# A hand-ordered attention and MLP block: another order for key sums, loads, scalings and weighings

## The chip, the cores and the metric

The kernel runs on one core of one Trainium2 chip. The metric is the time of one execution on the device in microseconds (us), the median of several runs. The core has five engines that run side by side, each working through its own instructions in order: TensorE (PE in the profile; its weight loads are PEld), VectorE (DVE), ScalarE (ACT), GpSimd (POOL) and SyncE (SP), which here only issues DMA transfers. They meet by semaphores.

## The reference

One token block of S = 2048 tokens and D = 576 features: a linear attention with 32 heads of 18 features, then an MLP with 4608 hidden features. All inputs are bf16.

```
x1 = layernorm(x)
q, k, v = heads(x1 @ wqkv)                       # 32 heads of 18
phi(t) = [softmax(t @ w_phi), softmax(-t @ w_phi)]     # 36 features a head
kv = sum over tokens of phi(k)^T v;   z = sum over tokens of phi(k)
o  = phi(q) kv / (phi(q) . z + 1e-6)
h  = x + o @ wo
y  = layernorm(layernorm(h))
out = h + gelu(y @ w1 + b1) @ w2 + b2
```

## The kernel before

**Tiles.** The 2048 tokens are 16 tiles of 128; two tiles make a pair p = 0 to 7, and the second index of most steps, i or a, picks a half of the heads or a tile of the pair. w_phi is folded into the key weights (wkp) and the query weights (wqp) on the chip, so that one product gives the logits.

**Order.** The scheduler is off: the body of the kernel is one long list of calls, and every engine runs its part of the list in the order in which it stands. So the list is at once the queue of each engine and of SP's DMA ring; an instruction that waits holds up all that stand behind it on its engine. TensorE's results go through a PSUM pool named `two` with three buffers in turn, so that a product can start only when the result three places back has been read.

**The steps that the change moves**, for a pair p:

- `load_x(t0, t1)`: SP loads tokens of x. `stats(p, i)`: VectorE's mean and variance. `power(p)`: GpSimd's 1/sqrt. `centre(p, i)`: GpSimd's shift, needed only where ACT scales. `scale(p, i, act or vec)`: the normalised tile, written by ACT (line 266) or VectorE (line 308). `turn_dma(p)`: SP transposes it by DMA (line 315) into lnT.
- `turn_wq(c)`: SP transposes chunk c of the query weights by DMA (line 368). `fold_mm("q", c)`, `fold_ev`: TensorE folds w_phi into it (line 393), ACT writes it to wqp (line 404). `swap_q(0 to 2)`: SP copies halves of wqp to the other 64 partitions (lines 408 to 412).
- `value_mm`, `key_mm`, `query_mm`: 18 matmuls each on 64 rows (line 423). `value_ev`: ACT's copy to vals (line 433). `key_exp`, `query_exp`: two exponentials each on ACT (line 445).
- `key_sum(p, i)`: VectorE's softmax denominators, a reduce and a reciprocal (lines 474, 476). `key_weigh(p, i, a, engine)`: phi(k) times the reciprocal (line 480), on GpSimd before. `query_sum`, `query_weigh`: the same for queries, into `padded` (lines 500 to 519). `turn_q(p)`: two DMA transposes of `padded` (line 545).
- `sums(p, a)`: eleven matmuls on 128 rows that add a tile's kv and z into `acc_kv` (line 559). All sixteen must be done ahead of `table`; `combine_mm` (line 644) then multiplies turned queries with the table, `divide` (lines 657, 658) divides.
- `load_wo(half)`: SP loads 64 partitions of wo (line 604), first used by `residual_mm` (line 693). `load_w1`, `load_w2`: the MLP's weights (lines 586, 592). The first quarter of w1 lies where the raw query and key weights lay.

SP's queue of before around the change is: `turn_dma(3)`, five `turn_wq`, `turn_dma(4)`, `load_x(12, 16)`, `turn_dma(5)`, `load_wo(0)`, three `swap_q`, two quarters' parts of w1, `turn_dma(6)`, `turn_dma(7)`, two parts of w1, `load_wo(1)`, `turn_q(0)`, and then w1 and w2 to the end.

After the attention of the first pair the MLP begins: `up` (line 1140, gelu in line 1162) and `down` (line 1184), with the later pairs' attention put between; the change leaves all that as it is.

Of the kernel before, what the change touches and what calls it, by code (L numbers as in the profile page):

```python
# [43 lines left out]
def kernel(  # L44
# [236 lines left out]
    def stats(p, i):  # L281
        if i == 0:
            moments[p] = [small.tile([P, 2, 2], FP32, name="mv", tag="mv")]
        mv = moments[p][0]
        st = small.tile([P, 2, nc.vector.BN_STATS_DIM], FP32, name="st", tag="st")
        for h in range(2):
            nc.vector.bn_stats(st[:, h, :], xh[:, 2 * p + i, h * HALF : (h + 1) * HALF])  # L287
        nc.vector.bn_aggr(mv[:, i, :], st[:, :, :])  # L288
        if i:
            moments[p] = [mv, None, None, None]  # L290

    def power(p):
        va = small.tile([P, 2], FP32, name="va", tag="va")
        nc.gpsimd.tensor_scalar(va[:, :], moments[p][0][:, :, 1], 1.0, EPS, ALU.mult, ALU.add)
        rs = small.tile([P, 2], FP32, name="rs", tag="rs")
        nc.gpsimd.tensor_tensor(rs[:, :], va[:, :], mhalf[:, 0:2], ALU.pow)
        moments[p][1] = rs
# [69 lines left out]
    def turn_wq(c):  # L367
        nc.sync.dma_start_transpose(wT[:, :, c * P : (c + 1) * P], wq[:, c, :])
# [119 lines left out]
    def key_sum(p, i):  # L488
        total("k", phik[p], p, i)

    def key_weigh(p, i, a, eng):
        weigh("k", phik[p], p, i, a, eng)
# [58 lines left out]
    def sums(p, a):  # L551
        t = 2 * p + a
        left.remove(t)
        for w in range(KW):
            n = COUNT[w]
            f0 = min(w * STEP, PW - P)
            b = w // 6
            at = (w - BANKS[b][0]) * WV
            nc.tensor.matmul(  # L559
                acc_kv[:, b, at : at + n * VW],  # L560
                phik[p][:, a, f0 : f0 + P],
                vals[:, t, FIRST[w] : FIRST[w] + n, :].rearrange("p h v -> p (h v)"),
                start=False, stop=not left, skip_group_check=True,
            )
# [285 lines left out]
    key_exp(1, 0)  # L850
    scale(3, 0, act)
    turn_dma(3)
    turn_wq(4)
    key_sum(0, 1)
    value_mm(0, 1)
    value_ev(0, 1, act)
    key_weigh(0, 0, 1, pool)
    key_weigh(0, 0, 0, pool)
    stats(4, 0)
    stats(4, 1)  # L860
    value_mm(1, 1)
# [2 lines left out]
    key_mm(2, 1)  # L864
    key_weigh(0, 1, 0, pool)
    key_weigh(0, 1, 1, pool)
    power(4)
    value_mm(1, 0)
    sums(0, 0)
    key_exp(2, 0)  # L870
    key_exp(2, 1)
    value_ev(1, 0, act)
    key_sum(2, 0)
    key_weigh(2, 0, 1, pool)
    stats(5, 0)
    stats(5, 1)
    power(5)
    scale(4, 1, vec)
    value_mm(2, 0)
    value_ev(2, 0, act)  # L880
    key_mm(1, 1)
    key_exp(1, 1)
    turn_wq(1)
    key_sum(2, 1)
    turn_wq(2)
    scale(4, 0, vec)
    centre(5, 1)
    scale(5, 1, act)
    value_mm(2, 1)
    value_ev(2, 1, act)  # L890
    key_mm(3, 0)
    key_exp(3, 0)
    value_mm(3, 0)
    key_weigh(2, 0, 0, pool)
    value_ev(3, 0, act)
    turn_wq(3)
    turn_wq(0)
    key_mm(3, 1)
    key_exp(3, 1)
    key_sum(1, 0)  # L900
    key_weigh(2, 1, 1, pool)
    sums(0, 1)
    value_mm(3, 1)
    turn_dma(4)
    value_ev(3, 1, act)
    fold_mm("q", 0)
    key_weigh(2, 1, 0, pool)
    key_weigh(1, 0, 1, pool)
    key_sum(1, 1)
    fold_ev("q", 0, act)  # L910
    sums(2, 0)
    key_weigh(1, 0, 0, pool)
    sums(2, 1)
    scale(5, 0, vec)
    key_weigh(1, 1, 1, pool)
    key_weigh(1, 1, 0, pool)
    key_sum(3, 1)
    fold_mm("q", 3)
    fold_ev("q", 3, act)
    load_x(12, 16)  # L920
    key_weigh(3, 1, 1, pool)
    fold_mm("q", 2)
    fold_ev("q", 2, act)
    stats(6, 0)
    key_sum(3, 0)
    key_weigh(3, 1, 0, pool)
    turn_dma(5)
    load_wo(0)
    value_mm(4, 1)
    value_ev(4, 1, act)  # L930
    fold_mm("q", 1)
    fold_ev("q", 1, act)
    key_weigh(3, 0, 1, pool)
    key_weigh(3, 0, 0, pool)
# [3 lines left out]
    key_exp(4, 0)  # L938
    key_sum(4, 0)
    power(6)  # L940
    fold_mm("q", 4)
    swap_q(2)
    fold_ev("q", 4, act)
    swap_q(0)
    key_mm(4, 1)
    sums(1, 0)
    key_exp(4, 1)
    key_sum(4, 1)
# [3 lines left out]
    key_mm(5, 1)  # L952
    key_exp(5, 0)
    key_exp(5, 1)
    key_sum(5, 1)
    load_w1(0, 4, syn)
    sums(3, 1)
    centre(6, 1)
    value_mm(4, 0)
    value_ev(4, 0, act)  # L960
    query_mm(0, 0)
    scale(6, 1, act)
    value_mm(5, 0)
    centre(6, 0)
    scale(6, 0, act)
    key_weigh(4, 0, 0, pool)
    key_weigh(4, 1, 1, pool)
    query_exp(0, 0)
    stats(7, 0)
    stats(7, 1)  # L970
    sums(4, 1)
    sums(3, 0)
    load_w1(0, 1, syn)
    value_ev(5, 0, act)
    key_weigh(4, 1, 0, pool)
# [2 lines left out]
    key_weigh(5, 1, 0, pool)  # L978
    key_sum(5, 0)
    query_exp(0, 1)  # L980
    sums(4, 0)
    key_weigh(5, 1, 1, pool)
    power(7)
    value_mm(5, 1)
# [2 lines left out]
    key_mm(6, 0)  # L987
    key_weigh(5, 0, 1, pool)
    value_ev(5, 1, act)
    centre(7, 1)  # L990
    scale(7, 1, act)
    query_sum(0, 0)
    scale(7, 0, vec)
    turn_dma(7)
    load_w1(0, 0, syn)
    key_weigh(5, 0, 0, pool)
    query_mm(3, 0)
    load_w1(0, 2, syn)
    query_weigh(0, 0, 1, pool)
    query_weigh(0, 0, 0, pool)  # L1000
    query_sum(0, 1)
# [1 line left out]
    key_sum(6, 0)  # L1003
    query_weigh(0, 1, 1, pool)
    key_mm(6, 1)
    sums(5, 1)
    value_mm(6, 0)
    query_exp(3, 0)
    query_weigh(0, 1, 0, pool)
# [1 line left out]
    key_exp(6, 1)  # L1011
    key_sum(6, 1)
    value_ev(6, 0, act)
    sums(5, 0)
    key_weigh(6, 1, 0, pool)
    key_weigh(6, 1, 1, pool)
# [10 lines left out]
    key_weigh(7, 0, 0, pool)  # L1027
    value_mm(7, 0)
    load_wo(1)
    key_weigh(7, 0, 1, pool)  # L1030
    key_sum(7, 1)
    key_weigh(7, 1, 0, pool)
    query_mm(4, 0)
    sums(6, 1)
    value_ev(7, 0, act)
    query_exp(4, 0)
    query_mm(7, 1)
    value_mm(7, 1)
    query_exp(7, 1)
    query_mm(2, 0)  # L1040
    sums(6, 0)
    value_ev(7, 1, act)
    sums(7, 0)
# [256 lines left out]
```

## Time and profile before

| | |
|---|---|
| median of 3 runs | 395.81 us (394.12 to 396.77) |
| profiled execution | 395.62 us, span 393.9 us |
| TensorE busy | 383.0 us (97%) |
| VectorE, ScalarE, GpSimd busy | 165.1, 161.8, 120.4 us |
| granted TensorE clock | 1.00 |
| moved by DMA | 35.43 MB |

The span runs from the first to the last instruction of one profiled execution; its time holds 1.7 us more. In a row of the timeline the columns are start and duration in us, engine and line, operation, what it writes from what it reads, shapes, count, and in brackets how long the engine idled before it and what ended that. Consecutive instructions of one kind are merged (x18 is eighteen). Matmuls are pipelined: the start of the next group tells more than a duration. A row of the waits has total us, times and the longest.

### The profile page before, as it was taken

How to read it: one execution, taken by the hardware profiler on the slowest of the kernel's cores; microseconds unless marked ns; L12 is line 12 of the kernel's file. 1: busy time of each engine (PE TensorE's matmuls, PEld its weight loads, DVE VectorE, ACT ScalarE, POOL GpSimd, SP SyncE). 2: the span in 40 equal slices, each digit the busy share in tenths (PEclk: the TensorE clock that was granted, in tenths of full speed). 3: DMA queues.
4: the chain of work that ended last, by engine and by line, in shares of the span. 5: the costliest groups of instructions: out<-in, count | busy, mean ns of one | idle time of the engine just before them, and what ended most of it. 6: DMA issues, size and time to landing. Idle time of an engine off the chain costs nothing.

```text
span 393.9 us, 10235 instructions
## 1 busy us (share of the span) xinstructions
PE 383.0 (97%) x4492; PEld 267.4 (68%) x4493; DVE 165.1 (42%) x371; ACT 161.8 (41%) x287; POOL 120.4 (31%) x160
## 2 busy tenths in 40 slices
PE   7999799999999999999999999999999999999997
PEld 4787577779977887854457887444577764447773
DVE  6997986486139568681009323000380000000100
ACT  4878677677600870036660000566400016661000
POOL 7289699314504355236002211000032110000120
PEclk9999999999999999999999999999999999999999
DMA  8889959999953656534004363000042000000000
GB/s 230 189 139 155 218 87 189 203 238 345 241 120 77 121 105 135 77 77 75 0 2 62 77 118 47 17 1 2 2 92 60 17 17 0 2 2 0 17 26 20
DMA packets 75084, 35.43 MB, mean 90 GB/s; under 512 B 63026, under 2 KB 72384, under 8 KB 74912
## 3 DMA queue, kind: packets, MB, share of 16 engines
q1 hardware_dynamic: 74352, 33.14, 40.8%
q0 software_dynamic: 400, 1.35, 1.4%
q8 instruction: 35, 0.57, 0.6%
q10 hardware_dynamic: 288, 0.30, 0.3%
q14 instruction: 9, 0.07, 0.1%
HBM read 17.20 MB, written 2.36 MB: 50 GB/s over the span
## 4 chain that ended last, share of the span: by engine, by line
PE 82%; DVE 7%; DMA 4%; SPq 2%; POOL 2%; issue 1%; ACT 1%; POOLq 0%; DVEq 0%
PE po L1184 35%; PE ph L1140 32%; PE pk L423 5%; PE pa L693 5%; PE pv L423 2%; DVE st L287 2%; DMA wqp<-wqp 2%; DMA w<-in_B_w_dram 2%; SPq L545 2%; PE pn L644 1%; PE acc_kv L559 1%; POOL padded L509 1%; DVE sk L474 1%; DVE shared L308 1%; DVE mv L288 1%
## 5 line engine op out<-in xcount | busy, mean ns | idle before, releaser
L1162 ACT ACTIVATE home<-ph,b1col 128x512 bf16<-128x512 f32 (+1 forms) x180 | 98.6, 599 | 170.8 <-PE ph L1140 167.7
L1184 PE MATMUL po<-w,home 128*128 128x288 bf16 (+2 forms) x1151 | 143.4, 286 | 0.4 <-DMA w<-in_B_w_dram 0.3
L1140 PE MATMUL ph<-shared,w 64*128 64x512 bf16 (+2 forms) x1638 | 141.5, 331 | 0.9 <-ACT home L1162 0.7
L1184 PEld LDWEIGHTS <-home 128*128 128x128 bf16 x1152 | 109.4, 98 | 32.6 <-issue 2.3
L1140 PEld LDWEIGHTS <-w 64*128 64x128 bf16 x1638 | 80.2, 94 | 61.0 <-issue 1.9
L1188 DVE TENSOR_TENSOR ot<-po,hb 128x288 bf16<-128x288 f32 (+2 forms) x32 | 14.5, 454 | 107.3 <-PE po L1184 101.4
L1173 POOL TENSOR_TENSOR hb<-xh,b2bc 128x576 f32<-128x576 bf16 x16 | 20.4, 1273 | 104.9 <-DVE ot L1188 95.5
L423 PEld LDWEIGHTS <-home 64*128 64x128 bf16 x864 | 42.6, 94 | 12.4 <-issue 3.0
L509 POOL TENSOR_TENSOR padded<-home,rq 128x540 bf16<-128x540 bf16 x32 | 34.8, 1102 | 39.8 <-DVE rq L501 17.5
L702 DVE TENSOR_TENSOR xh<-pa,xh 128x288 bf16<-128x288 f32 x32 | 13.2, 448 | 71.7 <-PE pa L693 71.7
L250 POOL TENSOR_TENSOR rs<-va,mhalf 128x1 f32<-128x1 f32 x16 | 8.8, 550 | 102.8 <-DVE va L248 102.8
L480 POOL TENSOR_TENSOR phik<-phik,rk 128x576 bf16<-128x576 bf16 x32 | 36.3, 1166 | 3.7 <-DVE rk L476 3.7
L474 DVE TENSOR_REDUCE sk<-phik 128x64 f32<-128x1152 bf16 x16 | 21.1, 1318 | 2.7 <-ACT phik L445 2.7
L423 PE MATMUL pk<-wqp,home 64*128 64x288 bf16 x288 | 20.1, 283 | 2.0 <-DMA wqp<-wqp 1.8
L445 ACT ACTIVATE home<-pk 128x576 bf16<-128x576 f32 x32 | 18.9, 648 | 7.7 <-PE pk L423 6.4
L500 DVE TENSOR_REDUCE sk<-home 128x64 f32<-128x1152 bf16 x16 | 21.0, 1313 | 0.0
L445 ACT ACTIVATE phik<-pk 128x576 bf16<-128x576 f32 x32 | 18.8, 652 | 4.3 <-PE pk L423 4.3
L423 PE MATMUL pk<-shared,home 64*128 64x288 bf16 x288 | 19.7, 283 | 0.7 <-ACT vals L433 0.4
L423 PE MATMUL pv<-wv,home 64*128 64x288 bf16 x288 | 20.3, 283 | 0.0
L657 DVE RECIPROCAL rec<-pn 128x18 f32<-128x18 f32 (+1 forms) x32 | 8.0, 249 | 28.9 <-PE pn L644 28.9
L693 PE MATMUL pa<-wo,shared 64*128 64x288 bf16 x288 | 18.8, 283 | 0.0
L693 PEld LDWEIGHTS <-shared 64*128 64x128 bf16 x288 | 13.9, 94 | 4.3 <-issue 0.5
(78 smaller groups left out, 199.9 us busy)
## 6 DMA issues: line engine op xcount, KB each, us to landing
w<-in_B_w_dram SPq DMA_DIRECT2D x21, 432.0 KB, 10.0
out_dram<-ot SPq DMA_DIRECT2D x15, 144.0 KB, 1.9
xh<-in_A_x_dram SPq DMA_DIRECT2D x3, 576.0 KB, 6.5
wo<-in_A_wo_dram SPq DMA_DIRECT2D x2, 648.0 KB, 8.9
w<-in_B_w_dram POOLq DMA_DIRECT2D x3, 432.0 KB, 11.6
wv<-in_A_wqkv_dram SPq DMA_DIRECT2D x2, 360.0 KB, 8.2
w<-in_A_wqkv_dram SPq DMA_DIRECT2D x4, 157.5 KB, 4.0
wv<-in_A_wqkv_dram SPq DMA_DIRECT2D x2, 288.0 KB, 9.3
```

The costliest lines, as they stand in the source:

```text
L423: nc.tensor.matmul(dst[:, a, 0:HALF], lhs[rows, c, :], w[rows, slot, i * HALF : (i + 1) * HALF], start=(n == 0), stop=(n == KC - 1),)
L445: nc.scalar.activation(rows[:, :, i * HH : (i + 1) * HH, s, :], flight[key, p, i][:, :, 0:HALF].rearrange("p a (h f) -> p a h f", f=DH), A ...
L474: nc.vector.tensor_reduce(sk[:, :, :], part_of(dst, i), AX.X, ALU.add)
L480: eng.tensor_tensor(part, part, flight["r" + key, p, i][:, a, :].rearrange("p (h o) -> p h o", o=1).to_broadcast([P, NH, DH]), ALU.mult,)
L500: nc.vector.tensor_reduce(sk[:, :, :], part_of(phiq[p], i), AX.X, ALU.add)
L509: eng.tensor_tensor(padded[:, a, g0 * P : (g0 + 5) * P].rearrange("p (g k) -> p g k", k=P)[:, :, 0:STEP].rearrange("p g (h f) -> p g h f", ...
L693: nc.tensor.matmul(pa[a], oT[p % 2][rows, c, :], wo[rows, c, cs], start=(c == 0), stop=(c == KC - 1),)
L1140: nc.tensor.matmul(ph[half][:, lo:hi], w1[p_ // 9][rows, c, p_ % 9 * P : (p_ % 9 + 1) * P], ln2T[rows, c, base + lo : base + hi], start=(c ...
L1162: nc.scalar.activation(hidden(m), ph[half][:, 0:width], AF.Gelu_apprx_tanh, bias=b1col[:, m : m + 1], scale=1.0,)
L1173: nc.gpsimd.tensor_tensor(hb[:, :], xh[:, t, :], b2bc[:, :], ALU.add)
L1184: nc.tensor.matmul(po[:, :], hidden(m)[:, i_ * P : (i_ + 1) * P], w2[m // 18][:, m % 18, cs], start=(j == 0), stop=(j == NM - 1),)
L1188: nc.vector.tensor_tensor(ot[:, cs], po[:, :], hb[:, cs], ALU.add)
```

## The change

Only the order of calls and the engine of some of them change; every product, sum and load stays. The key sums (`sums`) stand together in four places. `key_sum(1, 0)` and the weighings of p = 1 and 2 come earlier, ahead of `power(4)` and `power(5)`. The scalings `scale(5, 1)`, `scale(6, 0)` and `scale(7, 1)` go from ACT to VectorE, and their `centre` calls go; two weighings of p = 7 go from GpSimd to VectorE. On SP, `turn_wq` runs in the order 0, 3, 1, then `turn_dma(4)` and `load_x(12, 16)`, then 2 and 4; `load_wo(0)` goes from behind `turn_dma(5)` to behind `turn_dma(7)` and its two parts of w1.

```diff
--- before.py
+++ after.py
@@ -850,12 +850,12 @@
     key_exp(1, 0)
     scale(3, 0, act)
     turn_dma(3)
-    turn_wq(4)
     key_sum(0, 1)
     value_mm(0, 1)
     value_ev(0, 1, act)
     key_weigh(0, 0, 1, pool)
     key_weigh(0, 0, 0, pool)
+    key_sum(1, 0)
     stats(4, 0)
     stats(4, 1)
     value_mm(1, 1)
@@ -864,71 +864,67 @@
     key_mm(2, 1)
     key_weigh(0, 1, 0, pool)
     key_weigh(0, 1, 1, pool)
+    key_weigh(1, 0, 1, pool)
+    key_weigh(1, 0, 0, pool)
     power(4)
     value_mm(1, 0)
-    sums(0, 0)
     key_exp(2, 0)
+    value_ev(1, 0, act)
     key_exp(2, 1)
-    value_ev(1, 0, act)
     key_sum(2, 0)
     key_weigh(2, 0, 1, pool)
+    key_weigh(2, 0, 0, pool)
+    scale(4, 1, vec)
+    scale(4, 0, vec)
+    key_sum(2, 1)
+    key_weigh(2, 1, 1, pool)
+    key_weigh(2, 1, 0, pool)
     stats(5, 0)
     stats(5, 1)
     power(5)
-    scale(4, 1, vec)
+    turn_wq(0)
+    turn_wq(3)
+    turn_wq(1)
+    turn_dma(4)
+    load_x(12, 16)
+    turn_wq(2)
+    turn_wq(4)
     value_mm(2, 0)
     value_ev(2, 0, act)
     key_mm(1, 1)
     key_exp(1, 1)
-    turn_wq(1)
-    key_sum(2, 1)
-    turn_wq(2)
-    scale(4, 0, vec)
-    centre(5, 1)
-    scale(5, 1, act)
     value_mm(2, 1)
     value_ev(2, 1, act)
     key_mm(3, 0)
     key_exp(3, 0)
     value_mm(3, 0)
-    key_weigh(2, 0, 0, pool)
     value_ev(3, 0, act)
-    turn_wq(3)
-    turn_wq(0)
     key_mm(3, 1)
     key_exp(3, 1)
-    key_sum(1, 0)
-    key_weigh(2, 1, 1, pool)
+    sums(0, 0)
     sums(0, 1)
     value_mm(3, 1)
-    turn_dma(4)
     value_ev(3, 1, act)
     fold_mm("q", 0)
-    key_weigh(2, 1, 0, pool)
-    key_weigh(1, 0, 1, pool)
     key_sum(1, 1)
     fold_ev("q", 0, act)
-    sums(2, 0)
-    key_weigh(1, 0, 0, pool)
-    sums(2, 1)
     scale(5, 0, vec)
+    scale(5, 1, vec)
     key_weigh(1, 1, 1, pool)
     key_weigh(1, 1, 0, pool)
     key_sum(3, 1)
     fold_mm("q", 3)
     fold_ev("q", 3, act)
-    load_x(12, 16)
     key_weigh(3, 1, 1, pool)
-    fold_mm("q", 2)
-    fold_ev("q", 2, act)
     stats(6, 0)
     key_sum(3, 0)
     key_weigh(3, 1, 0, pool)
     turn_dma(5)
-    load_wo(0)
     value_mm(4, 1)
     value_ev(4, 1, act)
     fold_mm("q", 1)
+    fold_mm("q", 2)
+    fold_ev("q", 2, act)
     fold_ev("q", 1, act)
     key_weigh(3, 0, 1, pool)
     key_weigh(3, 0, 0, pool)
@@ -938,11 +934,14 @@
     key_exp(4, 0)
     key_sum(4, 0)
     power(6)
+    centre(6, 1)
     fold_mm("q", 4)
     swap_q(2)
     fold_ev("q", 4, act)
     swap_q(0)
     key_mm(4, 1)
+    sums(2, 0)
+    sums(2, 1)
     sums(1, 0)
     key_exp(4, 1)
     key_sum(4, 1)
@@ -952,24 +951,19 @@
     key_mm(5, 1)
     key_exp(5, 0)
     key_exp(5, 1)
+    scale(6, 0, vec)
     key_sum(5, 1)
     load_w1(0, 4, syn)
-    sums(3, 1)
-    centre(6, 1)
     value_mm(4, 0)
     value_ev(4, 0, act)
     query_mm(0, 0)
     scale(6, 1, act)
     value_mm(5, 0)
-    centre(6, 0)
-    scale(6, 0, act)
     key_weigh(4, 0, 0, pool)
     key_weigh(4, 1, 1, pool)
     query_exp(0, 0)
     stats(7, 0)
     stats(7, 1)
-    sums(4, 1)
-    sums(3, 0)
     load_w1(0, 1, syn)
     value_ev(5, 0, act)
     key_weigh(4, 1, 0, pool)
@@ -978,7 +972,6 @@
     key_weigh(5, 1, 0, pool)
     key_sum(5, 0)
     query_exp(0, 1)
-    sums(4, 0)
     key_weigh(5, 1, 1, pool)
     power(7)
     value_mm(5, 1)
@@ -987,15 +980,15 @@
     key_mm(6, 0)
     key_weigh(5, 0, 1, pool)
     value_ev(5, 1, act)
-    centre(7, 1)
-    scale(7, 1, act)
+    scale(7, 1, vec)
+    scale(7, 0, vec)
     query_sum(0, 0)
-    scale(7, 0, vec)
     turn_dma(7)
     load_w1(0, 0, syn)
     key_weigh(5, 0, 0, pool)
     query_mm(3, 0)
     load_w1(0, 2, syn)
+    load_wo(0)
     query_weigh(0, 0, 1, pool)
     query_weigh(0, 0, 0, pool)
     query_sum(0, 1)
@@ -1003,7 +996,6 @@
     key_sum(6, 0)
     query_weigh(0, 1, 1, pool)
     key_mm(6, 1)
-    sums(5, 1)
     value_mm(6, 0)
     query_exp(3, 0)
     query_weigh(0, 1, 0, pool)
@@ -1011,6 +1003,11 @@
     key_exp(6, 1)
     key_sum(6, 1)
     value_ev(6, 0, act)
+    sums(4, 1)
+    sums(3, 0)
+    sums(3, 1)
+    sums(4, 0)
+    sums(5, 1)
     sums(5, 0)
     key_weigh(6, 1, 0, pool)
     key_weigh(6, 1, 1, pool)
@@ -1027,17 +1024,17 @@
     key_weigh(7, 0, 0, pool)
     value_mm(7, 0)
     load_wo(1)
-    key_weigh(7, 0, 1, pool)
+    key_weigh(7, 0, 1, vec)
     key_sum(7, 1)
-    key_weigh(7, 1, 0, pool)
+    key_weigh(7, 1, 0, vec)
     query_mm(4, 0)
-    sums(6, 1)
     value_ev(7, 0, act)
     query_exp(4, 0)
     query_mm(7, 1)
     value_mm(7, 1)
     query_exp(7, 1)
     query_mm(2, 0)
+    sums(6, 1)
     sums(6, 0)
     value_ev(7, 1, act)
     sums(7, 0)
```

## The prediction

> **What bounds the kernel now.** I read the page first (busy shares, DMA slices), then TensorE's waits from 30 to 180 us, then the stretches of 10 us, then each engine's timeline from 15 to 73 us, where all moved lines run.
>
> ```profile
> PE 383.0 (97%) x4492; PEld 267.4 (68%) x4493; DVE 165.1 (42%) x371; ACT 161.8 (41%) x287; POOL 120.4 (31%) x160
> ...
> DMA  8889959999953656534004363000042000000000
> ...
> PE pk L423 <- DMA wqp<-wqp: 1.8, 1, 1.8
> ...
> PE acc_kv L559 <- POOL phik L480: 0.6, 1, 0.6
> PE pk L423 <- ACT vals L433: 0.4, 1, 0.4
> ...
> PE po L1184 <- DMA w<-in_B_w_dram: 0.3, 1, 0.3
> ```
>
> TensorE is busy for 97% of the span: the change can only win what TensorE idles, or what its own order costs. In the part that is reordered it idles three times for long, 2.8 us together; the largest wait is for the swap of the folded query weights (wqp). The last row of the waits lies behind the part: the last chunk of w2 lands when TensorE is already there.
>
> ```profile
> 40.00:50.00 10.00, 7.45 (x134) 5.66 (x132) 9.55 (x18) 6.79 (x13) 7.26 (x10) 1.00 1.07 218
> ...
> 60.00:70.00 10.00, 10.00 (x169) 7.85 (x167) 5.32 (x6) 7.78 (x14) 10.00 (x11) 1.00 1.11 210
> ...
> wo<-in_A_wo_dram SPq DMA_DIRECT2D x2, 648.0 KB, 8.9
> ```
>
> The page's DMA line has 40 slices of 9.85 us: the sixth (49 to 59) is half idle, the five behind it (59 to 108) are full. In the rows of two stretches of 10 us the last two columns are DMA share and GB/s; the last row is a half of wo. So a second bound runs beside TensorE: the transfers that SP issues from 57.84 on, which end with that chunk of w2.
>
> **Part 1, fewer visits to the key sums.**
>
> ```profile
> 23.38 1.28 PE L423 MATMUL pv<-wv,home 64*128 64x288 bf16 x18
> 24.60 0.48 PE L559 MATMUL acc_kv<-vals,phik 128*128 128x57 bf16 x11
> 25.01 1.27 PE L423 MATMUL pv<-wv,home 64*128 64x288 bf16 x18
> 26.12 1.26 PE L423 MATMUL pk<-shared,home 64*128 64x288 bf16 x18
> ...
> 34.86 0.69 PE L393 MATMUL pW<-w 128*128 128x126 bf16 x10
> ...
> 45.31 0.77 PE L423 MATMUL pk<-wqp,home 64*128 64x288 bf16 x9
> 47.88 0.77 PE L423 MATMUL pk<-wqp,home 64*128 64x288 bf16 x9 [1.80 <-DMA wqp<-wqp]
> 48.39 1.37 PE L423 MATMUL pv<-wv,home 64*128 64x288 bf16 x18
> ...
> 70.24 1.11 PE L559 MATMUL acc_kv<-vals,phik 128*128 128x57 bf16 x33
> ...
> 72.61 0.79 PE L644 MATMUL pn<-kvm,shared 128*128 128x57 bf16 x22
> ```
>
> From start to start, a block of 18 takes 1.11 us (25.01 to 26.12), but 1.22 ahead of a sum (23.38 to 24.60): 0.11 to go in. Thirty-three sum matmuls last 1.11, eleven 0.48: 0.32 for each eleven; from 24.60 to 25.01 are 0.41, so 0.09 to go out. A visit costs 0.20 beside its work. Before there are ten visits with a way in and out of their own (the pair of p = 2 stands between folds), after there are four: 6 x 0.20 = 1.2 us of TensorE, of which 1.0 lies ahead of the key blocks of p = 7.
>
> **Part 2, a new wait from ACT's order.** `value_ev(1, 0)` now stands ahead of `key_exp(2, 1)`.
>
> ```profile
> 22.50 2.30 ACT L445 ACTIVATE phik<-pk 128x576 bf16<-128x576 f32 x4 [0.29 <-PE pk L423]
> 24.70 0.64 ACT L433 CAST vals<-pv 128x576 bf16<-128x576 f32 x1
> ```
>
> ACT ran all four exponentials from 22.50 on. Now the last two wait for value block (1, 0), which ends at 24.66; behind the cast they end at about 26.4 instead of 24.8. `key_mm(1, 1)` takes the PSUM buffer of `key_mm(2, 1)` (three buffers in turn); without the sum ahead of it TensorE is there at 25.6. It waits 0.9. In exchange `scale(5, 1)` leaves ACT, and with it the casts are no longer late: the 0.4 of the waits goes.
>
> **Part 3, powers behind weighings, scalings on VectorE.**
>
> ```profile
> 20.64 4.53 POOL L480 TENSOR_TENSOR phik<-phik,rk 128x576 bf16<-128x576 bf16 x4 [0.53 <-DVE rk L476]
> ...
> 22.65 0.75 DVE L287 BATCH_NORM_STATS2 st<-xh 128x6 f32<-128x288 bf16 x2
> ...
> 23.56 0.77 DVE L287 BATCH_NORM_STATS2 st<-xh 128x6 f32<-128x288 bf16 x2
> ...
> 30.41 0.47 DVE L308 TENSOR_SCALAR shared<-xh,mv,rs 128x576 bf16<-128x576 bf16 x1
> 30.80 1.34 DVE L474 TENSOR_REDUCE sk<-phik 128x64 f32<-128x1152 bf16 x1
> ...
> 32.65 1.29 DVE L474 TENSOR_REDUCE sk<-phik 128x64 f32<-128x1152 bf16 x1
> ...
> 39.62 0.82 DVE L287 BATCH_NORM_STATS2 st<-xh 128x6 f32<-128x288 bf16 x2 [2.85 <-DMA xh<-in_A_x_dram]
> ```
>
> GpSimd weighs at 1.13 us each (4.53 / 4). With two more weighings ahead, `power(4)` (1.0, from the rows of `power(7)` in part 5) ends at 25.2 + 2.3 + 1.0 = 28.4; both scalings of p = 4 follow on VectorE (30.41 to 30.80: 0.4 each) to 29.4, where the second ended at 30.9 before. From 22.65 VectorE then has five key sums (30.80 to 32.65: 1.85 each), four statistics (22.65 to 23.56: 0.9 each) and four scalings before `stats(6, 0)`, with 0.3 of waiting for the power: 22.65 + 9.25 + 3.65 + 1.6 + 0.35 = 37.5, against 39.62.
>
> **Part 4, x ahead, and what is now behind it on SP.**
>
> ```profile
> 32.18 1.36 SPq L315 DMA_TRANSPOSE home<-shared  x1
> 33.59 0.58 SPq L173 DMA_DIRECT2D xh<-in_A_x_dram  x1
> ...
> DMA to landing us min/median/max: 2.4/6.0/11.6
> ...
> 40.76 2.07 PEld L423 LDWEIGHTS <-home 64*128 64x128 bf16 x36 [0.21 <-DMA home<-shared]
> ```
>
> `turn_dma(4)` moves from 32.18 to 29.5, the x load from 33.59 to 30.9. It took 6.0 to landing, the median of the x loads in the landing row (33.59 + 6.0 = 39.6, where VectorE's wait ended), so it lands at 36.9, ahead of VectorE's 37.5: the 2.85 of waiting is gone, `stats(6, 0)` is 2.1 earlier. But `turn_wq(2)` and `turn_wq(4)` are now queued behind the load. What a transpose behind it costs is in the last row: `turn_dma(5)`, the next in the queue, landed at 40.7, 1.1 after x. So chunk 2 comes at 37.7 (half a transpose less). TensorE comes to `fold_mm("q", 2)` at 36.3: 26.5, five blocks (5.5), the two sums of p = 0 with their way in and out (0.85), two blocks each with a way in (2.4), three folds (0.3 each by the row of ten, and 0.1 out). A new wait of 1.4 (0 if the transpose passes the load; 2.5 if x takes a us more).
>
> The swaps then leave behind the late fold, about 1.3 later than before, but no wo load is in front: its 648 KB (0.66 MB) at 218 GB/s held them for 3.0. They ended the wait at 47.88; I let them land at 47.9 + 1.0 - 3.0 = 45.9, by 1.0 since the last of the three leaves only 1.0 later. TensorE reaches the second half of `query_mm(0, 0)` at 46.1. The 1.8 is gone, with little to spare.
>
> TensorE's account: waits of 3.2 go (45.31 to 47.88 is 2.6 for nine matmuls that take 0.5 from 47.88 to 48.39, so 2.0; then 0.6, 0.4, and the 0.2 of the weight row at 40.76), 1.0 of visits goes, 0.9 and 1.4 come: the key blocks of p = 7 start 1.9 earlier, the first combination (72.61) could start 2.1 earlier.
>
> **Part 5, the last turn and wo behind it.**
>
> ```profile
> 53.22 0.19 POOL L294 TENSOR_SCALAR va<-mv 128x2 f32<-128x2 f32 x1
> ...
> 54.16 1.16 POOL L480 TENSOR_TENSOR phik<-phik,rk 128x576 bf16<-128x576 bf16 x1
> 55.30 0.27 POOL L260 TENSOR_SCALAR nb<-mv,rs 128x1 f32<-128x1 f32 x1
> ...
> 56.50 1.29 SPq L315 DMA_TRANSPOSE home<-shared  x1
> ...
> 57.84 1.26 SPq L586 DMA_DIRECT2D w<-in_B_w_dram  x2
> ...
> 62.63 6.29 SPq L545 DMA_TRANSPOSE shared<-padded  x2
> ...
> shared<-padded SPq DMA_TRANSPOSE x2, 7.8
> ```
>
> `scale(7, 1)` on ACT needed a shift that GpSimd ran behind a weighing (55.30); on VectorE both scalings follow the power (53.22 to 54.16, 1.0). The power comes at the end of GpSimd's row: `key_sum(3, 0)` ends 2.8 behind the start of `stats(6, 0)`, at 40.3, then two weighings, `power(6)`, one shift, six weighings, `power(7)`: 40.4 + 2.3 + 1.0 + 0.3 + 6.8 + 1.0 = 51.8. Two scalings: 52.7. So `turn_dma(7)` leaves at 52.8 instead of 56.50, 3.7 earlier, and the queue behind it starts 3.7 earlier, into an idle stretch. But it is longer by the first half of wo: 0.66 MB at 218 GB/s, 3.0 us (3.2 at 210; 0 if it fits into the idle stretch). I take 3.0, since from the start of this queue the DMA line shows no more gaps. `turn_q(0)` stands behind both halves of wo. Its two transposes were issued from 62.63 to 68.92 and took 7.8 to land in the mean; the second is what the combination at 72.61 needs, so there was no slack. It comes 3.7 - 3.0 = 0.7 earlier, TensorE is ready 2.1 earlier and waits the difference, 1.4, there. All transfers after it, up to the last chunk of w2, are in one full stream, 0.7 earlier too.
>
> The two weighings on VectorE (p = 7) have no row. 128x576 lies between a scaling of that size, 0.47, and a reduce of twice the size, 1.3; I take 0.8. They save GpSimd 2.3 us, and VectorE's idle time hides them: after the last key sum it waits for TensorE's sums. At 1.3 each `rk` of the last weighing would come 1.0 later, less than the 2.3 that GpSimd has won.
>
> The Trainium skill, "GPSIMD Engine Reference", Specifications, says that GpSimd shares SBUF interfaces with VectorE and contends with its instructions in a two-port mode or with two SBUF inputs: scalings and weighings on VectorE would slow the GpSimd row above. By that rule the queue would start up to 0.5 later for each scaling beside a weighing (below as a rival). The trace shows none of it so far:
>
> ```profile
> 29.59 10.13 POOL L480 TENSOR_TENSOR phik<-phik,rk 128x576 bf16<-128x576 bf16 x9
> ```
>
> Nine weighings in 10.13 are 1.13 each, with the scaling at 30.41 among them.
>
> **Sum.** The profiled execution took 395.62 (span 393.9 and 1.7 around it), 0.2 under the median of the runs. 395.62 - 0.7 = 394.9; at the median 395.1.
>
> **Rivals.**
> - *TensorE alone sets it.* The DMA stream keeps up, the combination starts 2.1 earlier, and w2 with it: 393.7. Without the two new waits of 0.9 and 1.4 as well, 391.4. For: DMA is half idle where wo now begins. Against: share 1.11 from 60 to 70.
> - *wo costs its whole length.* If GpSimd's or VectorE's row doesn't get earlier, `turn_dma(7)` stays near 56.5, and the stream is 3.0 late at `turn_q(0)` and at w2: 398.8. It is slower from `turn_dma(7)` after 53.5 on. For: it is a long chain, and each step of it was placed by hand. With 1 us more for the transposes behind two copies: 399.8.
> - *The x load holds the folds.* It is issued with transposes on both sides; another x load took 11.6 to landing (the row in part 4). Then chunk 2 lands at 43.6 instead of 37.7, TensorE loses 6 us more, and with 1.4 in hand and 0.7 won the time is about 400; it costs from the point where x takes over 7.4 us.
> - *Shared interfaces.* Scalings of p = 4 to 7 cost GpSimd four times 0.5: `turn_dma(7)` at 54.8, the stream 1.3 late: 397.1.
>
> **Chances.** Forecast (gain between 2 and -1) 0.55; TensorE alone 0.17, of which half beyond 391.8 (4 us); wo at whole length 0.14, a quarter of it beyond 399.8; x holding the folds 0.09; shared interfaces 0.05. A measurement of this kernel tells about 1% (4 us) from no change. So faster 0.09, slower 0.13, same 0.78. The range reaches from 392.4 (the first rival, between its two ends) to 398.8 (wo at whole length); the likeliest case alone has 393.8 to 396.8.
>
> **What would show it.** Right: TensorE waits for ACT's exponentials at about 25.6 and for the transposed weights at the third fold; no wait for wqp; no VectorE wait for x; `turn_dma(7)` near 52.8; a new wait of 1 to 2 us of the first combination for the transpose of `padded`; four groups of key sums. Wrong: `turn_dma(7)` after 54, a wait for wqp still there, or a combination that starts before 71 or after 73.5.

## The result, and the profile after

The change makes the kernel slower by a little: 396.98 us in the median of 20 runs (395.86 to 400.91) against 395.32 for the kernel before (20 runs, 393.86 to 398.00). The ratio is 1.0043, its 95% interval 1.0023 to 1.0063. The forecast was a gain of 0.7 us; 396.98 lies inside its range (392.4 to 398.8), but on the other side of no change. The profiled execution took 396.61 us, its span is 394.9 against 393.9.

First TensorE's waits from 20 to 120 us of the span; the columns are total us, times and the longest:

```profile
PE pn L644 <- DMA shared<-padded: 2.7, 1, 2.7
PE pb L749 <- DMA b1nat<-in_B_b_dram: 1.1, 1, 1.1
PE pW L393 <- DMA w<-w: 1.1, 2, 0.7
```

The wait for wqp is gone, and so are the waits of 0.6 and 0.4 listed below it. In their place stand three that end on transfers: the turned queries (`padded`) ahead of the first combination, the folded weights (`w<-w`), and b1. Next, the timelines of VectorE, SP and TensorE:

```profile
37.59 0.76 DVE L287 BATCH_NORM_STATS2 st<-xh 128x6 f32<-128x288 bf16 x2
...
53.08 1.28 SPq L315 DMA_TRANSPOSE home<-shared  x1
...
55.71 1.25 SPq L604 DMA_DIRECT2D wo<-in_A_wo_dram  x2
59.89 8.54 SPq L545 DMA_TRANSPOSE shared<-padded  x2
68.48 1.50 SPq L586 DMA_DIRECT2D w<-in_B_w_dram  x2
...
71.92 0.80 PE L644 MATMUL pn<-kvm,shared 128*128 128x57 bf16 x22 [2.69 <-DMA shared<-padded]
...
87.54 0.67 PE L1137 MATMUL ph<-shared,w 64*128 64x128 bf16 x17 [0.41 <-DVE shared L337]
```

VectorE comes to `stats(6, 0)` at 37.59 and waits for no x. `turn_dma(7)` is issued at 53.08, 3.4 earlier than before; the two transposes of `turn_q(0)` leave the queue at 68.43, 0.5 earlier; the first combination starts at 71.92, 0.7 earlier. Up to here the forecast holds. The first MLP matmul, though, starts at 87.54, and before it was this:

```profile
86.81 1.40 PE L1140 MATMUL ph<-shared,w 64*128 64x128 bf16 x40
```

So 0.7 earlier has become 0.7 later within 15 us. The chain that ended last names the transfers there (start, us):

```profile
70.02 14.65 DMA b1nat<-in_B_b_dram
...
84.72 0.19 PE pb L749
...
104.43 6.98 DMA w<-in_B_w_dram
111.46 4.45 PE po L1181 x35
```

b1, 9 KB (36x128 bf16), took 14.65 us to land. The last chunk of w2 lets TensorE go on at 111.46, where before it was 110.47: the 1.0 by which the span grew.

### The profile page after: what moved, and what is told of

The parts are those of the page before. It is cut to its first block, busy times and chain, and to the rows that moved or that the text cites. A ratio compares the mean times of both kernels' runs of the same rounds, so it can differ in the third digit from the quotient of the medians.

```text
span 394.9 us, 10227 instructions
## 1 busy us (share of the span) xinstructions
PE 381.9 (97%) x4492; PEld 266.4 (67%) x4493; DVE 168.9 (43%) x376; ACT 159.4 (40%) x284; POOL 118.6 (30%) x155
## 4 chain that ended last, share of the span: by engine, by line
PE 84%; DMA 7%; SPq 3%; POOL 2%; ACT 2%; issue 1%; DVE 0%; POOLq 0%
PE po L1181 35%; PE ph L1137 32%; PE pk L423 7%; PE pa L693 4%; PE pv L423 4%; DMA b1nat<-in_B_b_dram 4%; DMA w<-in_B_w_dram 2%; SPq L545 2%; PE acc_kv L559 1%; DMA w<-w 1%; ACT shared L386 1%; PE pn L644 1%; POOL padded L509 1%; SPq L592 1%; SPq L586 0%
## 5 line engine op out<-in xcount | busy, mean ns | idle before, releaser
L1137 PEld LDWEIGHTS <-w 64*128 64x128 bf16 x1638 | 78.4, 94 | 63.3 <-issue 1.8
L423 PEld LDWEIGHTS <-home 64*128 64x128 bf16 x864 | 43.8, 94 | 9.5 <-issue 0.8
L480 POOL TENSOR_TENSOR phik<-phik,rk 128x576 bf16<-128x576 bf16 x30 | 35.0, 1198 | 2.5 <-DVE rk L476 2.0
```

Source lines behind the costliest of these rows:

```text
L423: nc.tensor.matmul(dst[:, a, 0:HALF], lhs[rows, c, :], w[rows, slot, i * HALF : (i + 1) * HALF], start=(n == 0), stop=(n == KC - 1),)
L480: eng.tensor_tensor(part, part, flight["r" + key, p, i][:, a, :].rearrange("p (h o) -> p h o", o=1).to_broadcast([P, NH, DH]), ALU.mult,)
L1137: nc.tensor.matmul(ph[half][:, lo:hi], w1[p_ // 9][rows, c, p_ % 9 * P : (p_ % 9 + 1) * P], ln2T[rows, c, base + lo : base + hi], start=(c ...
```

## The experiments

Each kernel was timed beside the kernel before on the same chip, the change in 20 runs and the others in 5 to 12; all ratios are to the kernel before.

| edit | median us | ratio (95% interval) |
|---|---|---|
| the change | 396.98 | 1.0043 (1.0023 to 1.0063) |
| before, first half of wo late | 401.07 | 1.0157 (1.0125 to 1.0189) |
| before, first half of wo in the idle stretch | 396.84 | 1.0022 (1.0006 to 1.0039) |
| change, first half of wo where it was | 393.83 | 0.9952 (0.9933 to 0.9971) |
| change, first half of wo in the idle stretch | 391.50 | 0.9921 (0.9892 to 0.9949) |
| change, second half of wo behind `turn_q(0)` | 395.75 | 1.0000 (0.9978 to 1.0022) |
| change, biases early | 396.47 | 1.0044 (1.0013 to 1.0074) |
| change, halves of w1 exchanged | 396.30 | 1.0047 (1.0016 to 1.0077) |
| change, TensorE's idle time filled | 396.90 | 1.0027 (1.0008 to 1.0047) |
| the same, biases early | 396.01 | 1.0004 (0.9986 to 1.0023) |
| change, x behind both transposes | 400.52 | 1.0112 (1.0080 to 1.0144) |
| the same, biases early | 400.02 | 1.0097 (1.0067 to 1.0126) |
| idle-stretch version, biases early and halves exchanged | 394.06 | 0.9953 (0.9927 to 0.9979) |
| idle-stretch version, x behind both transposes | 392.77 | 0.9932 (0.9910 to 0.9954) |
| idle-stretch version, x behind one transpose | 392.42 | 0.9909 (0.9881 to 0.9938) |
| idle-stretch version, nine visits to the sums | 392.18 | 0.9923 (0.9897 to 0.9948) |
| idle-stretch version, weighings on GpSimd | 392.23 | 0.9936 (0.9915 to 0.9957) |

**Where the first half of wo stands.** Four kernels with one line moved: the kernel before with wo's move alone, the kernel before with wo behind `turn_dma(6)`, and the changed kernel with wo at its old place and behind `turn_dma(6)`.

```diff
 # kernel before
     turn_dma(5)
-    load_wo(0)
...
     load_w1(0, 2, syn)
+    load_wo(0)
```

> The kernel before with one part of the change: load_wo(0) behind turn_dma(7) and its two parts of w1. Theory C: the wait for wqp shrinks from 1.8 to under 0.5, but the stream is longer by 0.66 MB from 57.8 us on with no earlier start: turn_q(0) lands 2.5 to 3 us later, the last chunk of w2 too, 1.006 to 1.008 of the kernel before. Theory B: the gain at wqp shows, 0.996 to 1.000.

```diff
 # changed kernel (the kernel before likewise, from behind turn_dma(5))
     turn_dma(6)
+    load_wo(0)
...
     load_w1(0, 2, syn)
-    load_wo(0)
```

> The kernel before with one line moved: the first half of wo directly behind turn_dma(6), where the DMA engines are half idle; nothing else of the change. Theory A (place of wo alone is worth the difference): the wait of 1.8 for wqp is gone, the stream from 57.8 on is no later, 393 to 394 against 395. Theory B (the earlier place lets TensorE come too early to the transposes of padded, which stay where turn_dma(7) puts them, so 1 to 2 us of the gain return as a wait there): 394.5 to 396, with a wait of the combination of 1 us or more. The difference to 391.5 (changed kernel with wo in the same place) is what the rest of the change earns: 1.5 to 2.5 by A, over 3 by B.

> The changed kernel with load_wo(0) taken from behind w1(0, 2) to directly behind turn_dma(6), where DMA idles (50 to 54 us). Theory C: the stream from turn_dma(7) on is 3.0 us shorter, turn_q(0) lands near 69, the first combination starts at 69.0 to 69.6 instead of 71.9, the last chunk of w2 lands 2 to 3 us earlier: 0.996 to 0.998 of the kernel before. Theory B: the combination is earlier, but b1 stays behind w1(0, 5) and lands at 81 to 84, TensorE waits 3 to 4 us for it: 1.002 to 1.004.

```diff
 # changed kernel
     turn_dma(5)
+    load_wo(0)
...
     load_w1(0, 2, syn)
-    load_wo(0)
```

> The changed kernel with one line put back: the first half of wo again behind turn_dma(5), all else of the change kept. Theory A (the first half of wo in the full transfer stream is what turned the gain into a loss; it keeps turn_q(0) waiting 2.7 us): the swaps land by about 46, TensorE reaches them at about 46.1, so the wait for wqp stays under 0.6; no wait of the first combination, the last chunk of w2 lands about 3 us earlier than in the changed kernel, time 391.5 to 393. Theory B (wo's place doesn't matter, the reordered keys and VectorE's scalings cost the time): 396 to 397.5. Theory C (the wait for wqp simply comes back whole): wait 1.8, time 393 to 394.5.

With wo where it was, the rest of the change gains 0.48%, 1.9 us. That is the mechanism of theory A (no wait for wqp, none of the first combination), but not its 391.5 to 393: the third fold waited 2.4 there, see below. With wo behind `turn_dma(6)` the change gains 0.8%, more than theory C's 0.2 to 0.4%. This version and four variants of it further down (ratios 0.9909 to 0.9936, which the intervals don't tell apart) are the fastest of the study and beat both kernels. Its timeline of SP and TensorE:

```profile
53.26 1.29 SPq L315 DMA_TRANSPOSE home<-shared  x1
54.61 1.26 SPq L586 DMA_DIRECT2D w<-in_B_w_dram  x2
55.91 0.61 SPq L604 DMA_DIRECT2D wo<-in_A_wo_dram  x1
60.06 5.54 SPq L545 DMA_TRANSPOSE shared<-padded  x2
65.66 1.26 SPq L586 DMA_DIRECT2D w<-in_B_w_dram  x2
...
69.33 0.79 PE L644 MATMUL pn<-kvm,shared 128*128 128x57 bf16 x22
...
83.52 1.73 PE L1137 MATMUL ph<-shared,w 64*128 64x128 bf16 x46
```

`turn_dma(7)` is issued within 0.2 us of the changed kernel's, but the transposes of `padded` are out at 65.60 instead of 68.43, 2.8 earlier, the price of half of wo that the forecast put at 3.0. TensorE waits neither for `padded` nor for b1, the first combination is 2.6 earlier, the first MLP matmul 4.0 earlier. So one line of the change turned a gain into a loss. By itself that line costs the kernel before 1.6%, twice what theory C had. The good place alone makes the kernel before 0.2% slower, a little beyond theory B's 394.5 to 396, and by another wait than B's: the one for wqp goes, but TensorE then waits 2.5 us for GpSimd's weighings, and `turn_dma(7)` comes at 58.50. The gain of 0.8% needs the earlier rows of VectorE and GpSimd together with the load out of the full stream.

**What holds the transposes.** In 16 of the 18 profiles the second transpose of `padded` leaves SP 0.2 to 0.5 us behind the landing of the copy of wo queued ahead of it; in the two with x behind both transposes and wo in the stream it leaves 1.8 and 1.9 behind. The landings of wo (shortest, median, longest us from issue; two halves each) are these, for the changed kernel and then for the version with wo in the idle stretch:

```profile
DMA to landing us min/median/max: 10.1/10.9/11.7
```

```profile
DMA to landing us min/median/max: 6.0/7.7/9.3
```

The second half's: 56.4 + 11.7 = 68.1 against 68.43, and 55.91 + 9.3 = 65.2 against 65.60. To test it, the second half of wo went behind the transposes; the stream stays as long as it was.

```diff
-    load_wo(1)
...
     turn_q(0)
+    load_wo(1)
```

> The changed kernel with the second half of wo issued behind turn_q(0) instead of ahead of it; the stream has the same length. Theory b (the transposes of padded are held until the copy queued ahead has landed, 0.35 us before their issue ends): the second one's issue ends at about 66.2, 0.4 behind the landing of the first half of wo, it lands at about 69.5, TensorE's wait of 2.7 falls under 0.7, and the time to 395 to 396 (less if w2 is in time, more only if wo is late at the first residual). Theory d (the length of the stream is what costs): the wait goes, but comes back at b1 or at the last chunk of w2; 396.5 to 397.5.

```profile
54.03 1.28 SPq L315 DMA_TRANSPOSE home<-shared  x1
...
56.66 0.61 SPq L604 DMA_DIRECT2D wo<-in_A_wo_dram  x1
62.04 4.86 SPq L545 DMA_TRANSPOSE shared<-padded  x2
66.96 0.59 SPq L604 DMA_DIRECT2D wo<-in_A_wo_dram  x1
```

```profile
PE pW L393 <- DMA w<-w: 2.2, 1, 2.2
PE po L1181 <- DMA w<-in_B_w_dram: 0.9, 2, 0.6
```

`turn_dma(7)` is 1.0 later than in the changed kernel, and the transposes still leave 1.5 earlier. The wait for `padded` is gone, and the time is that of the kernel before, as theory b had it: 1.2 us by the medians and 1.7 by the ratios came back, so the copies ahead of the transposes are most of the loss against the kernel before. That the transposes wait for the landing, and not just for the time that the bytes ahead need, is what the 0.2 to 0.5 above speak for; this run doesn't separate the two. The idle-stretch version is still 4.3 us faster, and a wait of 0.9 for w2 appears, as theory d had it: the stream is no shorter.

**The x load and the stream's start.** With x behind both transposes, the third fold waits for nothing, but x comes later.

```diff
-    load_x(12, 16)
     turn_wq(2)
     turn_wq(4)
+    load_x(12, 16)
```

> The changed kernel with the last x load behind turn_wq(2) and turn_wq(4), wo as changed. Theory a (the third fold's wait, 0.6 or 2.4 from run to run, is what takes the forecast gain): no wait there, but x lands about 3 us later and the last scalings 1.2, as in the run with wo in the idle stretch; 395.5 to 396.3, runs close together. Theory d (the stream sets the combination and w2, whatever comes before): the stream begins 1.2 later, 397.5 to 398.5.

> The changed kernel with the x load behind both transposes and the biases loaded behind turn_dma(6); wo as changed. Theories a and c together: no wait of the third fold, none for b1; 394.8 to 395.6, the forecast's own number, runs within 1 us. Theory d: 396.5 to 398, with the combination's wait for padded at 2 us or more.

> The changed kernel with the first half of wo behind turn_dma(6), and the last x load issued behind turn_wq(2) and turn_wq(4) instead of ahead of them. Theory F (a transpose behind a copy waits for the copy's landing, which was the wait of 0.6 to 2.4 at the third fold): that wait is gone, x is issued about 2 us later and lands at about 37, when VectorE comes to it; 390.5 to 391.2, or 391.5 if the third fold waits for something else as long. Rival V (VectorE's row has no slack, so x later by 1 to 2 puts the scalings of p = 6 and 7 later and GpSimd's weighings with them): 391.8 to 393.

> The changed kernel with the first half of wo behind turn_dma(6) and turn_wq(2) alone ahead of the x load, turn_wq(4) behind it. Theory a: the third fold no longer depends on the copy, x is issued at 32.2 and lands ahead of 37.8, where VectorE comes to it (with both transposes ahead it landed at 38.9 and VectorE waited 1.3), so turn_dma(7) stays at 53.3: 390.5 to 391.3, runs within 1 us. Rival: the x load takes its landing time from the transposes around it wherever it stands and lands after 38.5: 392 to 393.

The timeline of VectorE in the third of these (wo in the idle stretch), and SP's timeline and TensorE's largest wait in the first:

```profile
38.92 0.82 DVE L287 BATCH_NORM_STATS2 st<-xh 128x6 f32<-128x288 bf16 x2 [1.32 <-DMA xh<-in_A_x_dram]
```

```profile
54.98 1.28 SPq L315 DMA_TRANSPOSE home<-shared  x1
...
61.78 9.89 SPq L545 DMA_TRANSPOSE shared<-padded  x2
```

```profile
PE pn L644 <- DMA shared<-padded: 5.2, 1, 5.2
```

VectorE waits 1.3 there and 1.4 in the first, where `turn_dma(7)` is 1.9 later than in the changed kernel and everything behind it slides: a wait of 5.2 and 3.5 us of time. With wo out of the stream the same edit costs 0.4 to 1.3 us (the ratios differ by 0.0011, the intervals overlap; the medians differ by 1.3), which is that run's rival V. Theories a and c of the first two runs fell. Theory d had the direction, but was 2 us short both times (400.5 and 400.0); the mean clock was 0.991 or less in all of these runs. So in the changed kernel what follows `turn_dma(7)` sets the time, and a wait of the third fold is cheap beside it. Behind one transpose, x was in time as theory a had it, the fold of the other chunk waited 2.0 instead, and the time, in the rival's range, isn't told apart from that of the idle-stretch version.

**The order behind the transposes.** Two edits of the changed kernel take the b1 wait away, and a third does both with wo in the idle stretch.

```diff
 # biases early
     turn_dma(6)
+    load_biases()
 # halves exchanged, for all six loads of the second quarter
-    load_w1(1, 0, syn)
-    load_w1(1, 1, pool)
+    load_w1(1, 0, pool)
+    load_w1(1, 1, syn)
```

> The changed kernel with the loads of b1 and b2 moved from behind turn_q(0) to behind turn_dma(6), into an idle stretch of DMA. Theory B (the late b1 alone costs the time): TensorE's wait of 1.1 us at the transpose of b1 goes and the whole rest comes 1.0 to 1.3 us earlier: 1.001 of the kernel before. Theory A or C (the stream of weight loads sets the end): the wait goes, but the last chunk of w2 still lands at 110.9 to 111.4 and TensorE waits there instead for 0.8 to 1.2 us: 1.003 to 1.004 of the kernel before.

> The changed kernel with the partition halves of the second w1 quarter exchanged between the two queues: GpSimd issues the parts for rows 0 to 63, SP those for rows 64 to 127. Same bytes, same places in the list. Theory A (two queues that write the same 64 rows share one rate of about 200 GB/s, two that write different halves reach 250 to 290): GpSimd's loads now run beside w1(0, 3) and w1(0, 5), which are rows 64 to 127, so from 72 to 84 us DMA moves over 250 GB/s, w1(0, 5) and b1 land before 80, the last chunk of w2 lands 1 to 1.7 us earlier, and the kernel is at 0.998 to 1.001 of the one before. Theory B: b1 is behind the same loads on SP; nothing is said of rates. Theory C (the 0.66 MB of wo moved into the full stretch): no change, 1.004.

> The changed kernel with the first half of wo behind turn_dma(6) (as in the run of that edit alone, 391.5), and beside it the biases loaded there too and the halves of w1's second quarter exchanged between SP and GpSimd. Theory S (with wo out of the full stream TensorE waits for no transfer behind 60 us, so a shorter or better mixed stream has nothing to give): 391.0 to 392.0. Rival R (the order of b1, b2 and w1 costs by itself, and was worth 0.5 to 1.5 in the two runs that changed it alone): 390.0 to 391.0.

In both single runs the b1 wait is gone from the profile, and the medians hardly move: 396.5 and 396.3. So the 1.1 for b1 is how that one execution lost its time; it isn't shown to be why the kernel is slower. With the biases early the ratio is that of theories A and C, but no wait for w2 took b1's place. With the halves exchanged 211 GB/s passed from 70 to 80 us, not theory A's 250. The two profiles don't show the edits alone, though: in both the third fold waited 2.4, so that TensorE came later, and these executions took 394.8 and 395.6, less than most runs of their kernels. The combined version lost 1.3 us by the ratios, 2.6 by the medians, against the idle-stretch version without them, where its theories had 390 to 392. In its profile wo, with the biases ahead of it, landed at 58.4, 5.2 later, and `turn_dma(7)`, a transpose behind it, landed at 59.4, 6.2 after its issue instead of 3.2. That looks like the hold again, one place earlier; no run tested it.

**TensorE's clock.** Of the 20 runs of the changed kernel, 17 had a mean granted clock of 0.996 or less; of the kernel before 3 of the 91 runs beside the experiments. The profile of the kernel before with wo late shows such drops, by stretches of its span; the last three columns are granted clock, DMA share and GB/s:

```profile
46.60:50.02 3.42, 1.53 (x36) 1.07 (x33) 3.25 (x9) 3.18 (x5) 3.42 (x4) 1.00 0.26 60
50.02:53.43 3.41, 3.41 (x34) 2.13 (x28) 3.27 (x5) 1.19 (x2) 3.24 (x6) 0.50 0.19 44
73.90:77.32 3.42, 1.46 (x34) 1.29 (x36) 0.73 (x3) 0.79 (x2) 0.93 (x2) 1.00 1.06 231
77.32:80.74 3.42, 3.42 (x32) 2.08 (x27) 1.85 (x7) 1.48 (x3) 0.00 (x0) 0.50 1.06 202
```

Twice a stretch of 3.41 us in which TensorE was busy for only 1.5 is followed by one at half the clock. All eight drops, in seven profiles, follow a stretch of this length with 1.53 us of work or less; after the stretch with 1.59 in the profile with the halves exchanged, and the one with 1.86 in that of the changed kernel, the clock stayed full. To see whether idle time does it, matmuls that nobody reads filled it, while the transfers stayed as they were:

```diff
 # in fold_mm, for chunk 2 of q
+            idle_work(flight[name, c][:, 0, :], 5)
 # in combine_mm, for the first combination
+                idle_work(whole[:, 0, :], 9)
 # idle_work: n times
+            nc.tensor.matmul(dst, ident, wide, start=True, stop=True)   # 128x512
```

> The changed kernel with the same filling matmuls (5 ahead of the third fold, 9 ahead of the first combination) and nothing else. Theory G and T (the clock drops come from the waits, but the last chunk of w2 holds TensorE at 111 us whatever the clock was before): clocks 0.999 to 1.000, the spread of the runs shrinks, median 396.2 to 396.8 (only the runs at 0.991 and under gain). Rival G alone (the transfers have slack, the half clock is the whole loss): 394.5 to 395.5.

> The changed kernel with the biases loaded early (as in the run with that edit alone, where no wait at w2 was left and the time was 396.5) and with idle time of TensorE filled: 5 matmuls of 128x512 that nobody reads ahead of the third fold, 9 ahead of the first combination, in the buffers that these then overwrite. The waits for the transfers themselves stay. Theory G (each wait of 2 us or more makes the chip grant half the clock for the next 3.41 us, at about 1.7 us each): mean granted clock 0.999 to 1.000 in nearly all runs instead of 0.991 to 0.996, median 394.8 to 395.4. Rival (the time is the waits alone, the clock follows nothing that TensorE does): clocks as before, 396.3 to 397.5, since the filler can only cost.

In both, 11 of 12 runs had the full clock, where it was 3 of 20 and 2 of 12 without the filler: idle time causes the drops. The time of the changed kernel stayed (396.90, where the theory with both causes had 396.2 to 396.8); with the biases early the ratio fell by 0.4% to that of the kernel before, though the intervals overlap, and 396.0 is above the 394.8 to 395.4 expected. The filler itself is not free:

```profile
71.78 2.12 PE L249 MATMUL pn<-ident 128*128 128x512 bf16 x9
73.74 0.78 PE L655 MATMUL pn<-kvm,shared 128*128 128x57 bf16 x22
```

It takes 2.0 us there, and no wait for `padded` is left, so part of it delays the combination. Kernels whose runs fell on both sides don't agree on a price: with wo at its old place four runs at 0.996 have a mean of 394.3 and three at full clock 393.6; in the kernel before with wo in the idle stretch six have 397.1 and six 396.2; with the weighings on GpSimd three have 394.2 and eight 392.3; but of the changed kernel itself nine at 0.995 or 0.996 have 396.5 and three at full clock 396.9. A run with a drop also has the wait that brought it, so none of these is the price of the clock alone, and at full clock the changed kernel is no faster. The Trainium skill, "TensorE: Matmul & The Clock Gate", Part 1, describes a gate that halves the clock by a free-running window of 3413 ns; the length agrees with the 3.41 here, but by that part an idle window is needed, and here 1.5 us of work in it did not prevent the drop.

**Two prices of the prediction.** Both on the idle-stretch version: the sums of the third group taken apart, and the two weighings back on GpSimd.

```diff
-    sums(3, 0)   # and 3,1  4,0  5,1  5,0: from the group behind sums(4, 1)
     value_mm(6, 1)
+    sums(3, 0)   # and so on, one each behind the next product
```

> The changed kernel with the first half of wo behind turn_dma(6), and the third group of key sums taken apart: of its six sums one stays, five stand alone behind value_mm(6,1), key_mm(7,0), key_mm(7,1), query_mm(7,0) and value_mm(7,0), so nine visits instead of four. Theory P (a visit costs TensorE 0.2 beside its work, as the prediction had it, and TensorE sets the end here): plus 1.0, 392.3 to 392.8. Rival N (what a visit costs is hidden in waits for exponentials and buffers): 391.3 to 391.8.

```diff
-    key_weigh(7, 0, 1, vec)
+    key_weigh(7, 0, 1, pool)
-    key_weigh(7, 1, 0, vec)
+    key_weigh(7, 1, 0, pool)
```

> The changed kernel with the first half of wo behind turn_dma(6), and the two weighings of p = 7 back on GpSimd. Theory W (GpSimd's row of weighings sets when the last key sums can run): the row is longer by two weighings of 1.13 less the 0.17 that each of six won't lose to VectorE any more, so 1.2 to 2.3; TensorE's wait for the last weighing grows from 0.4 to 1.5 to 2.5, and the time to 392.5 to 394. Rival H (the row has slack behind the last key blocks): 391.3 to 391.9, and the weighings beside VectorE back at 1.13.

TensorE's timeline with nine visits, and one row of the idle-stretch version with the group whole:

```profile
52.96 1.27 PE L423 MATMUL pv<-wv,home 64*128 64x288 bf16 x18
54.16 0.48 PE L559 MATMUL acc_kv<-vals,phik 128*128 128x57 bf16 x11
54.57 1.28 PE L423 MATMUL pv<-wv,home 64*128 64x288 bf16 x18
55.78 0.48 PE L559 MATMUL acc_kv<-vals,phik 128*128 128x57 bf16 x11
...
69.78 0.80 PE L644 MATMUL pn<-kvm,shared 128*128 128x57 bf16 x22
```

```profile
67.85 0.34 PE L559 MATMUL acc_kv<-vals,phik 128*128 128x57 bf16 x6 [0.42 <-POOL phik L480]
```

A block and a sum take 1.62 (54.16 to 55.78); a block alone takes 1.10 and eleven sums in a row of 66 a sixth of 1.99, 0.33: a visit costs 0.19, the prediction's 0.20. Five of them are 1.0, but the combination starts only 0.45 later (69.33 to 69.78), because the wait of 0.42 for GpSimd's last weighing went: TensorE and GpSimd are level there. The time hardly moved: the median of 392.2 lies between the two theories, the ratios are alike. GpSimd's rows, with two weighings on VectorE and with none (the second from the last run):

```profile
59.99 7.80 POOL L480 TENSOR_TENSOR phik<-phik,rk 128x576 bf16<-128x576 bf16 x6
```

```profile
60.08 9.01 POOL L480 TENSOR_TENSOR phik<-phik,rk 128x576 bf16<-128x576 bf16 x8
```

Six take 1.30 each beside VectorE's, eight 1.13 each alone: moving two wins 1.2 us of GpSimd's row, not 2.3, and 0.15% of the time (the intervals overlap). TensorE's wait for the last weighing grew from 0.4 to 0.6, not to theory W's 1.5 to 2.5.

## Why the prediction was wrong

**What held.** The waits that were to go went. VectorE was at `stats(6, 0)` at 37.59 (predicted 37.5), `turn_dma(7)` at 53.08 (52.8), the first combination at 71.92 (about 71.9). Its new wait for `padded` was 2.7 and not 1 to 2, since TensorE was ready 3.3 earlier instead of 2.1. The third and fifth fold waited 1.1 together (1.4). A visit cost 0.19 (0.20), half of wo 2.8 (3.0). That the rest of the change was worth 1.9 us with wo left in place, near the 2.1 of TensorE's row, is luck: in that profile the combination starts only 0.6 earlier (72.05), and most of the other 1.3 are waits for gelu and w2 behind 86 us that are gone.

**The step that failed** is the last of part 5: "All transfers after it, up to the last chunk of w2, are in one full stream, 0.7 earlier too." A stream that begins 0.5 to 0.7 earlier did not end earlier. From the transposes' end to the landing that lets TensorE into the last chunk of w2 the changed kernel took 43.0 us (68.43 to 111.46), the kernel before 41.6 (68.92 to 110.47). GB/s by stretches of 10 us from 70 to 90 show the place, first of the changed kernel, then of the kernel before:

```profile
70.00:80.00 10.00, 7.72 (x133) 6.08 (x135) 4.92 (x14) 4.43 (x8) 0.60 (x2) 1.00 1.03 210
80.00:90.00 10.00, 7.82 (x147) 6.33 (x145) 7.93 (x20) 7.07 (x14) 1.12 (x2) 1.00 1.04 207
```

```profile
70.00:80.00 10.00, 9.59 (x178) 7.32 (x175) 5.31 (x17) 5.88 (x10) 2.40 (x4) 1.00 1.04 197
80.00:90.00 10.00, 9.28 (x167) 7.61 (x162) 9.28 (x22) 8.00 (x16) 1.51 (x3) 1.00 1.04 251
```

The engines are full in all four rows, yet bytes pass at 197 to 251 GB/s, and in the same stretches of the idle-stretch version at 236 and 307. I took the rate of one stretch (218) for the whole stream and added and subtracted lengths. In the profiles late landings go with the moment at which GpSimd's loads of w1 join SP's. GpSimd's row in the changed kernel and before:

```profile
68.64 1.96 POOL L586 DMA_DIRECT2D w<-in_B_w_dram  x3 [1.02 <-PE acc_kv L559]
```

```profile
71.99 1.96 POOL L586 DMA_DIRECT2D w<-in_B_w_dram  x3 [1.54 <-ACT home L445]
```

They wait for TensorE's key sums in the first row and for ACT in the second. In the changed kernel they leave 0.2 us behind SP's first load of w1 there (68.48), before 3.0 us behind it (68.98). SP's second part of w1, behind which b1 stands in the queue, took 14.9 us to land in the first and 7.3 in the second. Over all 18 profiles it took 12.5 to 15.3 in the five with GpSimd's loads at most 0.6 us behind SP's or ahead of them; in the other thirteen, with 2.2 us or more between, 6.9 to 7.3, and 10.1 with the second half of wo just ahead of it. If this is the cause, TensorE's earlier row and the held transposes together brought the loss, by putting the two sets of loads side by side. No run moved GpSimd's loads alone, so it isn't shown.

**The term behind it** is the 3.0 for half of wo, which 3.7 of earlier start was to pay for. Its size in the queue was right, 2.8. As a price of the move it was about right against the old place (3.1 us by the medians, 3.6 by the ratios) and too small against the idle stretch (5.5 and 4.8). The rest lies with what follows it, not divided by any run: held transposes, late w1 and w2, half a clock. The rival "wo costs its whole length" had the loss, but not its condition: it is slower "from `turn_dma(7)` after 53.5 on", and the kernel was slower with 53.08 already. With 54.98, in the run with x behind both transposes, it took 400.5, beyond the rival's 398.8 and 399.8.

**Smaller misses.** The 0.9 of waiting for ACT's exponentials did not occur: TensorE went on at 25.45 without a gap. Part 4 priced the transpose behind the x load as one number; it is two, see below. The two weighings on VectorE took 1.6 and 0.9 us each, not 0.8 and at most 1.3. The rival of shared interfaces was right in kind for weighings (1.30 against 1.13); the Trainium skill's sentence that GpSimd contends with VectorE's instructions of two SBUF inputs ("GPSIMD Engine Reference", Specifications) agrees with that.

**What stays open.** How the loss divides between clock and stream isn't settled, since the filler cost time itself. The changed kernel has one profile, at full clock, where most of its runs were below; whether b1 and w1 were late in those too isn't known.

## What to carry to other kernels

A load moved off one wait belongs where the DMA engines are idle, not merely where the waiting engine doesn't look: the same 0.66 MB cost about 5 us more in a full queue than in a half-empty stretch. Before moving a copy in a queue, look for the next transpose behind it: here that one left the queue only behind the copy's landing, and all that is queued after it left later still. Bring back the parts of a change one at a time: here the place of one load hid a gain of 0.8%.

## What the runs showed of the hardware

The second transpose of `padded`, behind copies in SP's queue, came out 0.2 to 0.5 us behind their landing in 16 of 18 profiles. For `turn_wq(2)` behind the x load the profiles show one of two delays. The timelines of SP and TensorE in the changed kernel and in the one with the biases early, whose order is the same up to there (x took 4.6 to land in both):

```profile
30.79 0.58 SPq L173 DMA_DIRECT2D xh<-in_A_x_dram  x1
...
36.12 0.44 PE L393 MATMUL pW<-w 128*128 128x126 bf16 x5 [0.65 <-DMA w<-w]
```

```profile
31.59 0.58 SPq L173 DMA_DIRECT2D xh<-in_A_x_dram  x1
...
38.49 0.44 PE L393 MATMUL pW<-w 128*128 128x126 bf16 x5 [2.44 <-DMA w<-w]
```

The fold starts 0.7 behind x's landing in the first (35.4) and 2.3 behind it in the second (36.2). Nothing here shows what decides. TensorE's granted clock fell to half for 3.41 us, twice for 6.83, after stretches of 3.41 us with 1.53 us of work or less, and after none with 1.59 or more; with the idle time filled it stayed full in 11 of 12 runs.
